# Weight conversions spread over more slots, a low part moved by half an iteration, and output copies moved behind multiplies, in a fused attention and feed-forward kernel

## The chip, the cores and the metric

The kernel runs on one core of one Trainium2 chip. The metric is the device time of one execution in microseconds (us); lower is better. Times are medians of several executions of the same kernel on the same chip.

## The reference

The input is attention data (4 batches, 8 heads, 768 positions, 64 channels), and the output has 3072 rows of 512 numbers. Weights arrive as 64-bit floats and are used as 32-bit floats.

```
for each chunk of 32 queries:
    keys, values = 8 memory rows + 16 rows to the left, the chunk, 8 rows to the right
    a = softmax(q k^T / sqrt(64));  out = a v
x  = out, heads side by side                  # 3072 x 512
h  = x @ w_in                                 # 512 -> 2048
g  = where(h > 0, h, exp(min(h, 0)) - 1)
x1 = g @ w_out                                # 2048 -> 512
y  = ((x1 @ w1) * (x1 @ w2)) @ w3 @ w_out2    # 512 -> 1024, product, 1024 -> 1024 -> 512
```

## The kernel before

**Numbers in two parts.** Every operand of a multiply is held as a high part (`hi`, the value rounded to TensorE's reduced 32-bit form, made by ScalarE with a cast) and a low part (`lo`, the value less `hi`, made by VectorE with a subtraction that reads the cast's result). A product is three multiplies, hi·hi, hi·lo and lo·hi (`mm3`, lines 124 to 126).

**The main loop.** The 3072 rows are cut into 8 blocks of 384. For each block j there are 16 iterations, one per 128 columns of w_in; n counts all 128 iterations. In iteration n TensorE makes `mm_h(n)` (twelve multiplies, h into one of two PSUM banks that alternate, lines 124 to 126 with `xhl`) and `mm_x(n-2)` (twelve multiplies, g into four banks, the same lines with `g`). Between them ScalarE makes relu and exp of h (L539, L540), VectorE the maximum that gives g (`elu_max`, L545, which is also the last reader of the h bank), ScalarE the cast of g (`elu_hi`, L549) and VectorE the low part (`elu_lo`, L553). The order on each engine is the order of the program text: each engine takes its instructions one after another, and one that has to wait holds up all behind it.

**Slots.** Twice per iteration `at_step` runs what a table has put into that slot, so there are 32 slots per block. Since iteration 16 these hold two things. One is attention for the blocks to come, in groups G of 128 queries, three per block, by the list `chain` and the slot offsets "slow": `at_first` (every sixth group, memory keys), `at_turn` (transposes of q and k into the PSUM tile PA, L305 and L307), scores, max, sum, norm, flip, values, `at_out` (cast L120 and low part L121 of the block's input `xhl`, read from PA). The other is the preparation of the second network's weights (`Job`, `plan`): raw 64-bit words are loaded, `rebase` (ScalarE, L159), `shift` (VectorE, L163) and `low` (VectorE, L167) make a 32-bit float tile of 128x512, and it is stored to DRAM as hi and lo. There are 8 tiles of w_out2 (`wos`), 16 of w3 (`w3s`), which TensorE also transposes into PA first (`mid_flip`, L419), and 8 pairs of w1 and w2 tiles (`duos`), each of which gives four stored tiles, two of them from differences (`duo_first`, `duo_second`). Hi and lo of these are made by L172 and L175, and by L438 and L439 for the pairs. The two buffers `st` hold what is about to be stored; `store_next`, at the next slot, issues the store on the SP queue, which also carries the raw loads and those of q, k and v.

In the loop over G (after `GM`), a group that is not the first of its block takes a pair while there are any, and otherwise a w_out2 tile; most groups take a w3 tile too. So the pairs are done in the first four of the six blocks (n = 16 to 111, blocks 1 to 6) in which groups are worked on. The last block (block 7) has none.

**The last stage.** A fold of w3 and w_out2 follows, and then 32 iterations, `mm_step`, eight for each of four pairs of blocks. Each makes seven half products of 6 multiplies (`mm_half`, L661 to L663) by a scheme with sums and differences, whose results alternate between the banks y and z, and six `mm_o` of the iteration before (3 multiplies of 512 columns each) into six accumulators: four banks, and for output tiles 4 and 5 the two halves of PA. ScalarE and VectorE (`sub`, L443) make c11 and c22 of the half products; their product's casts (L699) and low parts feed the next iteration's `mm_o`. In the first iteration of a pair the accumulators of the pair before are finished, and `store_out` copies each to SBUF (even tiles on ScalarE, L115; odd ones on VectorE, L117) and stores it. `do(t)` runs `between[t]`, which is `behind`: `mm_o(n - 1, t)` and, in that iteration, `store_out(p - 1, t)`:

```
        mm_half(n, y, "a22", "t4", False, True)
        do(4)
        do(5)
        sub(c11, c11, c12, ALU.mult)
        sub(c22, y, c22, ALU.mult)
```

Of the kernel before, what the change touches and what calls it, by code (L numbers as in the profile page):

```python
# [8 lines left out]
F32 = mybir.dt.float32  # L9
# [10 lines left out]
def tile_kernel(  # L20
# [23 lines left out]
    nc = tc.nc  # L44
# [371 lines left out]

    def mid_flip(job):
        for i in range(KT):
            nc.tensor.transpose(PA[:, 0, i * P:(i + 1) * P], job.f[:, i * P:(i + 1) * P], ident)  # L419
        mid_split(job, PA[:, 0, :])  # L420

    class Duo:

# [5 lines left out]
        def block(self, i, k):  # L429
            return self.jobs[i].f[:, k * 256:(k + 1) * 256]  # L430

        def keep(self, r, fill):
            w = self.stores[r].shape[2]
            part = Job(None, store=self.stores[r])
            part.to = pools["st"].tile([P, 2, 512], F32R, tag="st", name="st")[:, :, 0:w]
            t = part.to[:, 1, :].bitcast(F32)
            src = fill(t)
            nc.scalar.copy(part.to[:, 0, :], src)  # L438
            nc.vector.tensor_tensor(out=part.to[:, 1, :], in0=src, in1=part.to[:, 0, :].bitcast(F32), op=ALU.subtract)  # L439
            stores.append(part)  # L440
# [5 lines left out]
    def duo_plain(duo):  # L446
        duo.keep(0, lambda t: duo.jobs[0].f)

    def duo_first(duo):
        def fill(t):  # L450
            sub(t[:, 0:256], duo.block(1, 0), duo.block(0, 0))
            sub(t[:, 256:512], duo.block(1, 1), duo.block(1, 0))
            return t

        duo.keep(1, fill)

    def duo_second(duo):
        def fill(t):
            sub(t[:, 256:512], duo.block(1, 1), duo.block(1, 0))
            sub(t[:, 0:256], t[:, 256:512], duo.block(0, 0), ALU.add)  # L460
            sub(t[:, 256:512], duo.block(0, 1), t[:, 0:256])
            return t

        duo.keep(2, fill)

    def duo_last(duo):
        duo.keep(3, lambda t: duo.block(1, 1))

    def store_next():
        while stores:  # L470
# [24 lines left out]
    def plan(s0, job, *steps):  # L495
        mid_jobs.append(job)
        for at, fn in steps:
            put(s0 + at, fn, job)

    for G in range(GPB, NG):  # L500
# [5 lines left out]
        if G % GPB and duos:  # L506
            duo = duos.pop(0)
            plan(s0, duo.jobs[0], (0, rebase), (1, mid_low))
            plan(s0, duo.jobs[1], (2, rebase), (3, mid_low))
# [76 lines left out]
    def fill(slot, src):  # L586
        nc.sync.dma_start(out=W[slot].bitcast(F32), in_=src)
# [77 lines left out]
    def acc(t):  # L665
        return PS[t] if t < KT else PA[:, t - KT, :]

    def mm_step(n, last, between):

        y, z = PS[4][:, 0:TB], PS[5][:, 0:TB]  # L670
        if last:
            for i in sorted(between):
                between[i]()
            return
        r1, r2, r5, c11, c12, c22 = (e_f[i] for i in range(6))
        do = lambda i: between[i]() if i in between else None
# [12 lines left out]
        sub(c22, y, r5, ALU.add)  # L689
        do(3)  # L690
        mm_half(n, z, "s4", "b22", False, True)
        sub(c12, z, r2, ALU.add)
        mm_half(n, y, "a22", "t4", False, True)
        do(4)
        do(5)
        sub(c11, c11, c12, ALU.mult)
        sub(c22, y, c22, ALU.mult)
        for r, e in enumerate((c11, c22)):
            nc.scalar.copy(gq[2 * (n % 2) + r][:, 0, :], e)  # L699
        for r, e in enumerate((c11, c22)):  # L700
            g = gq[2 * (n % 2) + r]
            sub(g[:, 1, :], e, g[:, 0, :].bitcast(F32))
# [15 lines left out]
    with tc.manual_schedule():  # L718
# [40 lines left out]
        for n in range(NH + 2):  # L759
            j, f, at, last = seq[n] if n < NH else (NB, n - NH, n - NH, False)  # L760
            first = at < 2 and n >= 2
            if j == NB - 1 and f == 0:
                store_next()
                mid_ctx.close()
                at_ctx.close()
                late = ctx.enter_context(tc.tile_pool(name="late", bufs=1, side="right"))
                more = [late.tile([P, 2, 2, TB], F32R, name=f"xc{i}") for i in range(3)]
                left.append({})
                for i, what in enumerate(LEFTS[:4]):
                    left[0][what] = [xhl[i // 2][:, r, i % 2 * 2:i % 2 * 2 + 2, :] for r in range(2)]  # L770
                for i, what in enumerate(LEFTS[4:]):
                    left[0][what] = [more[i][:, r] for r in range(2)]
            if n == FF1:
                feed.until(len(feed.jobs) - 1)
                raw_ctx.close()
                mid_ctx = ExitStack()
                pools["raw"] = mid_ctx.enter_context(tc.tile_pool(name="raw2", bufs=2, side="right"))
                pools["st"] = mid_ctx.enter_context(tc.tile_pool(name="st_p", bufs=2, side="right"))
                mid_load(2)

            def x():
                if n >= 2:
                    if n < FF1 + 2:
                        feed.until(due[FF1 + seq[n - 2][1]])
                    mm_x(n - 2)
                    if at == 1 and n < NH:
                        store_x1(j - 1)
                if n < FF1:
                    feed.step()
                at_step()  # L790

            if first:
                x()
            if n < NH:
# [66 lines left out]
        for n in range(NA + 1):  # L861
            p, f = divmod(n, FF2)

            def behind(t, n=n, p=p, f=f):
                if t == 0 and n < NA and p + 1 < NPAIR and f >= 1:
                    left_step(p + 1, f - 1)
                if n >= 1:
                    mm_o(n - 1, t)
                    if f == 0:
                        store_out(p - 1, t)  # L870

            mm_step(n, n == NA, {t: lambda t=t: behind(t) for t in range(2 * GPB)})
# [34 lines left out]
```

## Time and profile before

| what | value |
|---|---|
| median of 3 executions | 1132.85 us (1131.69 to 1133.08) |
| the profiled execution, its own time | 1132.95 us |
| its span, first to last instruction | 1131.1 us |
| TensorE multiplies busy | 1062.1 us, 94% |
| VectorE busy | 593.2 us, 52% |
| ScalarE busy | 461.3 us, 41% |
| instructions in the span | 20839 |

The profile is of one execution. The span is shorter than the time by what lies before the first and after the last instruction. PE is TensorE, DVE is VectorE, ACT is ScalarE, SP is the engine that issues transfers. A line number such as L553 is the line of the kernel; where a helper records an operation, all of its uses share that line. Names such as `xhl<-banks` say which tile an instruction writes and which it reads. An idle time is given with the instruction that ended it.

### The profile page before, as it was taken

How to read it: one execution, taken by the hardware profiler on the slowest of the kernel's cores; microseconds unless marked ns; L12 is line 12 of the kernel's file. 1: busy time of each engine (PE TensorE's matmuls, PEld its weight loads, DVE VectorE, ACT ScalarE, POOL GpSimd, SP SyncE). 2: the span in 40 equal slices, each digit the busy share in tenths (PEclk: the TensorE clock that was granted, in tenths of full speed). 3: DMA queues.
4: the chain of work that ended last, by engine and by line, in shares of the span. 5: the costliest groups of instructions: out<-in, count | busy, mean ns of one | idle time of the engine just before them, and what ended most of it. 6: DMA issues, size and time to landing. Idle time of an engine off the chain costs nothing.

```text
span 1131.1 us, 20839 instructions
## 1 busy us (share of the span) xinstructions
PE 1062.1 (94%) x8528; PEld 996.0 (88%) x8528; DVE 593.2 (52%) x1080; ACT 461.3 (41%) x965; POOL 1.7 (0%) x16
## 2 busy tenths in 40 slices
PE   4788899899899899899999999999999999999998
PEld 4688799799799899799999999789989998998997
DVE  4898566566666566565565334134443443354333
ACT  3667555455455454455444443122222222222122
POOL 0000000000000000000000000000000000000000
PEclk9799999999999999999999999999999999999999
DMA  8947355555554545553421675365465465455531
GB/s 191 297 141 199 94 150 148 161 152 174 163 155 139 166 147 177 162 152 111 139 73 35 196 252 186 129 185 161 152 219 193 144 214 201 148 173 177 177 94 57
DMA packets 170090, 180.40 MB, mean 159 GB/s; under 512 B 101388, under 2 KB 140300, under 8 KB 169996
## 3 DMA queue, kind: packets, MB, share of 16 engines
q1 hardware_dynamic: 168956, 178.81, 51.3%
q8 instruction: 67, 1.10, 0.4%
q10 hardware_dynamic: 1040, 0.26, 0.1%
q14 instruction: 27, 0.22, 0.1%
HBM read 139.20 MB, written 39.85 MB: 158 GB/s over the span
## 4 chain that ended last, share of the span: by engine, by line
PE 62%; DVE 18%; ACT 13%; issue 4%; DMA 3%; DVEq 0%; SPq 0%; ACTq 0%
PE bank L124 11%; PE bank L125 11%; PE bank L126 11%; PE bank L661 7%; PE bank L662 7%; PE bank L663 7%; ACT g L549 3%; DVE eg L545 3%; PE banks L124 2%; DVE e L366 2%; PE banks L126 2%; PE banks L125 2%; DVE pT L377 1%; DVE g L553 1%; ACT eg L540 1%
## 5 line engine op out<-in xcount | busy, mean ns | idle before, releaser
L124 PE MATMUL bank<-xhl,w 128*128 128x384 f32 x512 | 178.7, 349 | 16.4 <-DVE eg L545 15.6
L124 PE MATMUL bank<-g,w 128*128 128x384 f32 x512 | 176.0, 344 | 2.8 <-ACT g L549 2.8
L125 PE MATMUL bank<-xhl,w 128*128 128x384 f32 x512 | 172.8, 337 | 0.9 <-DVE xhl L121 0.9
L126 PE MATMUL bank<-xhl,w 128*128 128x384 f32 x512 | 172.7, 337 | 0.0
L125 PE MATMUL bank<-g,w 128*128 128x384 f32 x512 | 172.1, 336 | 0.3 <-DVE g L553 0.3
L126 PE MATMUL bank<-g,w 128*128 128x384 f32 x512 | 172.0, 336 | 0.0
L549 ACT CAST g<-eg 128x384 fp32r<-128x384 f32 x128 | 65.9, 515 | 168.8 <-DVE eg L545 168.8
L553 DVE TENSOR_TENSOR g<-eg,g 128x384 fp32r<-128x384 f32 x128 | 71.4, 558 | 98.0 <-ACT g L549 98.0
L124 PEld LDWEIGHTS bank<-xhl,w 128*128 128x128 f32 x512 | 97.2, 190 | 24.3 <-DVE eg L545 21.2
L124 PEld LDWEIGHTS bank<-g,w 128*128 128x128 f32 x512 | 96.7, 189 | 4.4 <-ACT g L549 3.2
L125 PEld LDWEIGHTS bank<-xhl,w 128*128 128x128 f32 x512 | 97.2, 190 | 1.3 <-DVE xhl L121 1.3
L125 PEld LDWEIGHTS bank<-g,w 128*128 128x128 f32 x512 | 96.8, 189 | 1.0 <-DVE g L553 1.0
L126 PEld LDWEIGHTS bank<-xhl,w 128*128 128x128 f32 x512 | 97.1, 190 | 0.0
L126 PEld LDWEIGHTS bank<-g,w 128*128 128x128 f32 x512 | 96.5, 189 | 0.0
L545 DVE SCALAR_TENSOR_TENSOR eg<-eg,bank 128x384 f32<-128x384 f32 x128 | 69.6, 544 | 42.9 <-ACT eg L540 42.9
L443 DVE TENSOR_TENSOR e<-bank,e 128x384 f32<-128x384 f32 x64 | 35.4, 554 | 104.9 <-PE bank L663 61.5
L443 DVE TENSOR_TENSOR e<-bank,eg 128x384 f32<-128x384 f32 x64 | 35.7, 558 | 91.8 <-PE bank L663 91.8
L539 ACT ACTIVATE eg<-bank 128x384 f32<-128x384 f32 x128 | 62.7, 490 | 50.7 <-PE bank L126 50.7
L699 ACT CAST g<-e 128x384 fp32r<-128x384 f32 x64 | 31.4, 513 | 126.3 <-DVE e L443 126.3
L661 PE MATMUL bank<-xd,w 128*128 128x384 f32 x224 | 76.1, 340 | 3.5 <-DVE e L443 3.5
L662 PE MATMUL bank<-xd,w 128*128 128x384 f32 x224 | 76.7, 342 | 0.0
L663 PE MATMUL bank<-xd,w 128*128 128x384 f32 x224 | 76.4, 341 | 0.0
(143 smaller groups left out, 1870.9 us busy)
## 6 DMA issues: line engine op xcount, KB each, us to landing
w<-wqd SPq DMA_DIRECT2D x96, 512.0 KB
raw<-in_moe_w_dram SPq DMA_DIRECT2D x32, 512.0 KB
wqd<-st SPq DMA_DIRECT2D x24, 512.0 KB
raw<-in_moe_w_out_dram SPq DMA_DIRECT2D x20, 512.0 KB
w3d<-st SPq DMA_DIRECT2D x16, 512.0 KB
w<-w3d SPq DMA_DIRECT2D x16, 512.0 KB
w<-wqd SPq DMA_DIRECT2D x32, 256.0 KB
raw<-in_moe_w_in_dram SPq DMA_DIRECT2D x12, 512.0 KB
```

Source lines behind the costliest of these rows:

```text
L124: mm(o, lhsT=w_hi, rhs=x_hi, start=start, stop=False)
L125: mm(o, lhsT=w_hi, rhs=x_lo, start=False, stop=False)
L126: mm(o, lhsT=w_lo, rhs=x_hi, start=False, stop=stop)
L443: nc.vector.tensor_tensor(out=o, in0=a, in1=b, op=op)
L539: nc.scalar.activation(e, h_t[n], AF.Relu, scale=-1.0)
L545: nc.vector.scalar_tensor_tensor(out=e, in0=e, scalar=-1.0, in1=h_t.pop(n), op0=ALU.add, op1=ALU.max)
L549: nc.scalar.copy(g_t[n][:, 0, :], eg_t[n])
L553: nc.vector.tensor_tensor(out=g[:, 1, :], in0=eg_t.pop(n), in1=g[:, 0, :].bitcast(F32), op=ALU.subtract)
L661: mm(o, lhsT=args[0], rhs=args[2], start=start and i == 0, stop=False, skip_group_check=more)
L662: mm(o, lhsT=args[0], rhs=args[3], start=False, stop=False, skip_group_check=more)
L663: mm(o, lhsT=args[1], rhs=args[2], start=False, stop=i == 1, skip_group_check=more)
L699: nc.scalar.copy(gq[2 * (n % 2) + r][:, 0, :], e)
```

## The change

Four things are edited; no operation is added or left out.

1. `shift` is no longer part of `mid_low`, and hi and lo of a converted tile are separate steps: `mid_hi`, `mid_lo`, `mid_flip_lo`, and for the pairs `Duo.hi` and `Duo.lo`. The two differences now only write `duo.next`; their hi and lo follow as steps.
2. The slots are written out anew (`plan_duo` and the two `plan` lines), and the list DUOS says which groups, counted from the first, take a pair: over all six blocks. The other groups take w_out2 tiles.
3. `elu_lo` of iteration n-1 comes in iteration n, behind the first slot, instead of directly behind `elu_hi`.
4. In the last stage, copies and stores of output tiles 4 and 5 come behind both `mm_o` and behind c22 and c11, which are exchanged. At the very end tile 5 is stored before tile 4.

```diff
     def mid_low(job):
-        shift(job)
         low(job)
         mid_load(mid_jobs.index(job) + 3)
 
-    def mid_split(job, src=None):
-        job.to = pools["st"].tile([P, 2, 512], F32R, tag="st", name="st")
+    def mid_hi(job, src=None):
+        job.to = st_tile()
         hi_of(job, src)
-        lo_of(job, src)
+
+    def mid_lo(job):
+        lo_of(job)
         stores.append(job)
 
     def mid_flip(job):
         for i in range(KT):
             nc.tensor.transpose(PA[:, 0, i * P:(i + 1) * P], job.f[:, i * P:(i + 1) * P], ident)
-        mid_split(job, PA[:, 0, :])
+        mid_hi(job, PA[:, 0, :])
+
+    def mid_flip_lo(job):
+        lo_of(job, PA[:, 0, :])
+        stores.append(job)
...
-            for at, fn in ((2, duo_plain), (7, duo_first), (8.5, duo_last), (9.5, duo_second)):
-                put(s0 + at, fn, duo)
...
+    def plan_duo(s0, duo):
+        plan(s0, duo.jobs[0], (-1, rebase), (0.1, shift), (0.2, mid_low))
+        plan(s0, duo.jobs[1], (1, rebase), (1.3, shift), (2.3, mid_low))
...
+            (10.3, duo_second), (10.4, lambda d: d.hi(2)), (11.1, Duo.lo),
...
+    DUOS = (1, 2, 4, 7, 10, 11, 13, 16)
...
         elif wos:
-            plan(s0, wos.pop(0), (0, rebase), (1, mid_low), (2, mid_split))
-        if w3s and (not G % GPB or len(duos) % 4 < 3):
-            plan(s0, w3s.pop(0), (4, rebase), (5, mid_low), (9, mid_flip))
+            plan(s0, wos.pop(0), (2, rebase), (3.5, shift), (4.5, mid_low), (5.1, mid_hi), (6.1, mid_lo))
+        if w3s and G - GM not in (2, 11):
+            plan(s0, w3s.pop(0), (5, rebase), (6.2, shift), (7.6, mid_low), (9.1, mid_flip), (9.6, mid_flip_lo))
...
+        def do(i):
+            between[i]()
+            if i < 4:
+                stored(i)
+
...
         do(4)
         do(5)
+        sub(c22, y, c22, ALU.mult)
         sub(c11, c11, c12, ALU.mult)
-        sub(c22, y, c22, ALU.mult)
+        stored(4)
+        stored(5)
...
             at_step()
             if spread:
                 elu_exp(n)
+            if FF1 < n < NH:
+                elu_lo(n - 1)
             if not first:
                 x()
             if n < NH:
                 elu_max(n)
             if n < NH and not spread:
                 elu_hi(n)
-                elu_lo(n)
+                if n == NH - 1:
+                    elu_lo(n)
```

How the instructions stand now, at three places. Lines have moved by some: L545 is now L555, L553 is L563, L439 of the pairs is L175, L443 is L455.

VectorE, third group of block 1, from the transpose of the softmax (L377) on; L545 is elu_max, L553 the lo of g, L121 the lo of the attention output, and the `st` rows are the pair and the flipped w3 tile. Before:

```order
L377 STREAM_TRANSPOSE pT<-e_2440 128x1024
L443 TENSOR_TENSOR st<-f 128x256 x2
L439 TENSOR_TENSOR st<-st 128x512
L545 SCALAR_TENSOR_TENSOR eg<-eg,bank_95 128x384
L553 TENSOR_TENSOR g<-eg,g 128x384
L121 TENSOR_TENSOR xhl_73<-banks,xhl_73 128x2x4x64
L439 TENSOR_TENSOR st<-f,st 128x256
L175 TENSOR_TENSOR st<-banks,st 128x512
L443 TENSOR_TENSOR st<-f 128x256
L443 TENSOR_TENSOR st<-st,f 128x256
L443 TENSOR_TENSOR st<-f,st 128x256
L439 TENSOR_TENSOR st<-st 128x512
```

and with the change:

```order
L377 STREAM_TRANSPOSE pT<-e_2454 128x1024
L455 TENSOR_TENSOR st<-f 128x256 x2
L563 TENSOR_TENSOR g<-eg,g 128x384
L175 TENSOR_TENSOR st<-st 128x512
L555 SCALAR_TENSOR_TENSOR eg<-eg,bank_95 128x384
L121 TENSOR_TENSOR xhl_73<-banks,xhl_73 128x2x4x64
L563 TENSOR_TENSOR g<-eg,g 128x384
L555 SCALAR_TENSOR_TENSOR eg<-eg,bank_96 128x384
L455 TENSOR_TENSOR st<-f 128x256
L455 TENSOR_TENSOR st<-st,f 128x256
L455 TENSOR_TENSOR st<-f,st 128x256
L175 TENSOR_TENSOR st<-st 128x512
```

The lo of g now stands ahead of the max instead of behind it, there is no flip in this group, and the block's last max (bank_96) stands ahead of the second difference instead of behind it.

ScalarE, block 1, from the end of its first group to the turn of its second (L309 copies the turned q); L120 is the cast of the attention output, `st<-banks` the cast of the flipped w3 tile, L159 a rebase. Before:

```order
L120 CAST xhl_73<-banks 128x2x4x64
L549 CAST g<-eg 128x384
L539 ACTIVATE eg<-bank_96 128x384
L540 ACTIVATE eg<-eg 128x384
L172 CAST st<-banks 128x512
L309 COPY qT<-banks 128x512
```

and with the change:

```order
L120 CAST xhl_73<-banks 128x2x4x64
L559 CAST g<-eg 128x384
L549 ACTIVATE eg<-bank_96 128x384
L550 ACTIVATE eg<-eg 128x384
L159 ACTIVATE f<-raw 128x512
L172 CAST st<-banks 128x512
L309 COPY qT<-banks 128x512
```

The rebase of the next pair's first tile now stands ahead of the flip's cast.

VectorE, first iteration of a pair in the last stage; `st<-banks` is the copy of output tile 5, `e_8035` is c11, `e_8037` is c22, bank_95 is y. Before:

```order
L117 COPY st<-banks 128x512
L443 TENSOR_TENSOR e_8035<-e_8035,e_8036 128x384
L443 TENSOR_TENSOR e_8037<-bank_95,e_8037 128x384
L443 TENSOR_TENSOR g<-e_8035,g 128x384
L443 TENSOR_TENSOR g<-e_8037,g 128x384
```

and with the change:

```order
L455 TENSOR_TENSOR e_8037<-bank_95,e_8037 128x384
L455 TENSOR_TENSOR e_8035<-e_8035,e_8036 128x384
L117 COPY st<-banks 128x512
L455 TENSOR_TENSOR g<-e_8035,g 128x384
L455 TENSOR_TENSOR g<-e_8037,g 128x384
```

c22, the last reader of y, and then c11 now stand ahead of the copy.

## Rows read from the trace of the kernel before

**Rows 1.** The page, first part: busy time, share of the span, instructions.

```profile
PE 1062.1 (94%) x8528; PEld 996.0 (88%) x8528; DVE 593.2 (52%) x1080; ACT 461.3 (41%) x965; POOL 1.7 (0%) x16
```

**Rows 2.** Table by stage, blocks 1-7: length; PE, PEld, DVE, ACT, POOL; clock; DMA.

```profile
132.62:213.91 81.29, 78.63 (x803) 75.26 (x801) 49.85 (x95) 41.97 (x93) 0.00 (x0) 1.00 0.50 151
213.91:299.52 85.61, 80.08 (x810) 75.51 (x809) 53.84 (x104) 43.27 (x93) 0.00 (x0) 1.00 0.54 163
299.52:382.45 82.93, 78.86 (x802) 75.17 (x801) 52.23 (x100) 42.60 (x94) 0.00 (x0) 1.00 0.51 153
382.45:467.96 85.51, 80.34 (x809) 75.46 (x808) 53.77 (x103) 43.10 (x93) 0.00 (x0) 1.00 0.54 163
467.96:549.57 81.61, 79.44 (x807) 76.87 (x805) 47.13 (x88) 40.52 (x90) 0.00 (x0) 0.98 0.46 135
549.57:628.45 78.88, 78.19 (x805) 75.33 (x805) 41.57 (x77) 37.23 (x82) 0.00 (x0) 1.00 0.27 76
628.45:694.90 66.45, 66.45 (x385) 66.45 (x385) 21.20 (x37) 27.09 (x53) 0.00 (x0) 1.00 0.70 234
```

**Rows 3.** TensorE's waits, 132.6 to 628.5: us in total, times, longest.

```profile
PE banks L419 <- DVE xhl L121: 6.4, 4, 1.6
PE bank L124 <- DVE eg L545: 5.9, 11, 0.8
PE banks L305 <- ACT memo L300: 3.8, 2, 2.2
PE bank L124 <- ACT g L549: 2.8, 2, 1.6
PE banks L305 <- DVE st L175: 0.6, 3, 0.2
```

**Rows 4.** Waits of all engines, whole span, same columns.

```profile
DVE g L553 <- ACT g L549: 98.0, 114, 3.6
```

**Rows 5.** Timeline, end of block 1: start, us, instruction, idle time before it.

```profile
208.03 0.55 DVE L545 SCALAR_TENSOR_TENSOR eg<-eg,bank 128x384 f32<-128x384 f32 x1
...
208.61 0.51 ACT L549 CAST g<-eg 128x384 fp32r<-128x384 f32 x1 [1.22 <-DVE eg L545]
...
210.58 0.69 DVE L121 TENSOR_TENSOR xhl<-banks,xhl 128x512 fp32r<-128x512 f32 x1 [0.86 <-ACT xhl L120]
...
211.32 0.33 PE L419 MATMUL banks<-ident,f 128*128 128x128 f32 x1 [1.61 <-DVE xhl L121]
```

**Rows 6.** Timeline, turn of a second group (block 2); then L159's group.

```profile
244.08 0.33 PE L305 MATMUL banks<-ident,qn 128*128 128x128 f32 x1 [0.20 <-DVE st L175]
...
L159 ACT ACTIVATE f<-raw 128x512 f32<-128x512 f32 x64 | 42.9, 670 | 0.4 <-DMA raw<-in_moe_w_dram 0.4
```

**Rows 7.** Table by stage: iterations of the last stage at pair boundaries, and one plain.

```profile
831.55:846.02 14.47, 11.98 (x61) 10.48 (x60) 5.20 (x10) 3.69 (x8) 0.00 (x0) 0.98 0.52 197
846.02:860.45 14.43, 14.43 (x61) 13.47 (x61) 5.09 (x10) 3.64 (x8) 0.00 (x0) 0.79 0.66 221
860.45:872.00 11.55, 11.55 (x61) 10.75 (x60) 4.61 (x10) 3.15 (x6) 0.00 (x0) 1.00 0.48 159
944.24:957.47 13.23, 13.23 (x61) 12.43 (x61) 5.09 (x10) 3.64 (x8) 0.00 (x0) 0.87 0.75 239
1041.26:1052.92 11.66, 11.66 (x60) 10.86 (x61) 4.22 (x9) 2.92 (x7) 0.00 (x0) 1.00 0.79 270
```

**Rows 8.** Timeline at the first pair boundary.

```profile
842.65 0.59 ACT L115 COPY st<-banks 128x512 f32<-128x512 f32 x1 [4.02 <-PE banks L126]
...
843.29 0.51 PE L124 MATMUL banks<-w,g 128*128 128x512 f32 x1 [0.72 <-ACT st L115]
...
844.34 0.69 DVE L117 COPY st<-banks 128x512 f32<-128x512 f32 x1 [2.91 <-PE banks L126]
...
846.02 0.69 PE L661 MATMUL bank<-xd,w 128*128 128x384 f32 x1 [1.77 <-DVE e L443]
```

**Rows 9.** Timeline, last output tile.

```profile
1126.54 0.50 PE L124 MATMUL banks<-w,g 128*128 128x512 f32 x1 [0.72 <-ACT st L115]
```

More of the change, by code (lines that the diff above doesn't have):

```diff
@@ L406, in mid_low, with st_tile @@
     def mid_low(job):
-        shift(job)
         low(job)
         mid_load(mid_jobs.index(job) + 3)
-    def mid_split(job, src=None):
-        job.to = pools["st"].tile([P, 2, 512], F32R, tag="st", name="st")
+    def st_tile(w=512):
+        return pools["st"].tile([P, 2, 512], F32R, tag="st", name="st")[:, :, 0:w]
+    def mid_hi(job, src=None):
+        job.to = st_tile()
         hi_of(job, src)
-        lo_of(job, src)
+    def mid_lo(job):
+        lo_of(job)
         stores.append(job)
@@ L430, in block, with hi, lo @@
             return self.jobs[i].f[:, k * 256:(k + 1) * 256]
-        def keep(self, r, fill):
+        def hi(self, r, src=None):
             w = self.stores[r].shape[2]
[L434 to L440, printed above, removed]
+            self.part = Job(None, store=self.stores[r])
+            if src is None:
+                self.part.to, src = self.next, self.next[:, 1, :].bitcast(F32)
+            else:
+                self.part.to = st_tile(w)
+            self.src = src
+            hi_of(self.part, src)
+        def lo(self):
+            lo_of(self.part, self.src)
+            stores.append(self.part)
     def sub(o, a, b, op=ALU.subtract):
@@ L444, in sub @@
         return o
-    def duo_plain(duo):
-        duo.keep(0, lambda t: duo.jobs[0].f)
     def duo_first(duo):
[L450 to L455, printed above, removed]
-    def duo_second(duo):
[L458 to L467, printed above, removed]
+        duo.next = st_tile()
+        t = duo.next[:, 1, :].bitcast(F32)
+        sub(t[:, 0:256], duo.block(1, 0), duo.block(0, 0))
+        sub(t[:, 256:512], duo.block(1, 1), duo.block(1, 0))
+    def duo_second(duo):
+        duo.next = st_tile()
+        t = duo.next[:, 1, :].bitcast(F32)
+        sub(t[:, 256:512], duo.block(1, 1), duo.block(1, 0))
+        sub(t[:, 0:256], t[:, 256:512], duo.block(0, 0), ALU.add)
+        sub(t[:, 256:512], duo.block(0, 1), t[:, 0:256])
     def store_next():
@@ L498, in plan @@
             put(s0 + at, fn, job)
+    def plan_duo(s0, duo):
+        plan(s0, duo.jobs[0], (-1, rebase), (0.1, shift), (0.2, mid_low))
+        plan(s0, duo.jobs[1], (1, rebase), (1.3, shift), (2.3, mid_low))
+        for at, fn in (
+            (1.2, lambda d: d.hi(0, d.jobs[0].f)), (2.2, Duo.lo),
+            (4.5, lambda d: d.hi(3, d.block(1, 1))), (5.1, Duo.lo),
+            (6.8, duo_first), (6.9, lambda d: d.hi(1)), (7.5, Duo.lo),
+            (10.3, duo_second), (10.4, lambda d: d.hi(2)), (11.1, Duo.lo),
+        ):
+            put(s0 + at, fn, duo)
+    DUOS = (1, 2, 4, 7, 10, 11, 13, 16)
     for G in range(GPB, NG):
@@ L505, in tile_kernel @@
             continue
[L506 to L509, printed above, removed]
-            for at, fn in ((2, duo_plain), (7, duo_first), (8.5, duo_last), (9.5, duo_second)):
-                put(s0 + at, fn, duo)
+        if G - GM in DUOS:
+            plan_duo(s0, duos.pop(0))
         elif wos:
-            plan(s0, wos.pop(0), (0, rebase), (1, mid_low), (2, mid_split))
-        if w3s and (not G % GPB or len(duos) % 4 < 3):
-            plan(s0, w3s.pop(0), (4, rebase), (5, mid_low), (9, mid_flip))
+            plan(s0, wos.pop(0), (2, rebase), (3.5, shift), (4.5, mid_low), (5.1, mid_hi), (6.1, mid_lo))
+        if w3s and G - GM not in (2, 11):
+            plan(s0, w3s.pop(0), (5, rebase), (6.2, shift), (7.6, mid_low), (9.1, mid_flip), (9.6, mid_flip_lo))
     assert not wos and not w3s and not duos, (len(wos), len(w3s), len(duos))
@@ L666, in acc, with mm_step @@
         return PS[t] if t < KT else PA[:, t - KT, :]
-    def mm_step(n, last, between):
+    def mm_step(n, last, between, stored):
         y, z = PS[4][:, 0:TB], PS[5][:, 0:TB]
@@ L673, in mm_step @@
                 between[i]()
+                if i != 4:
+                    stored(i)
+            stored(4)
             return
         r1, r2, r5, c11, c12, c22 = (e_f[i] for i in range(6))
-        do = lambda i: between[i]() if i in between else None
+        def do(i):
+            between[i]()
+            if i < 4:
+                stored(i)
         mm_half(n, y, "a11", "b11", True, True)
@@ L695, in mm_step @@
         do(5)
+        sub(c22, y, c22, ALU.mult)
         sub(c11, c11, c12, ALU.mult)
-        sub(c22, y, c22, ALU.mult)
+        stored(4)
+        stored(5)
         for r, e in enumerate((c11, c22)):
@@ L868, in behind, with stored @@
                     mm_o(n - 1, t)
-                    if f == 0:
-                        store_out(p - 1, t)
-            mm_step(n, n == NA, {t: lambda t=t: behind(t) for t in range(2 * GPB)})
+            def stored(t, p=p, f=f, n=n):
+                if n >= 1 and f == 0:
+                    store_out(p - 1, t)
+            mm_step(n, n == NA, {t: lambda t=t: behind(t) for t in range(2 * GPB)}, stored)
             if n < NA:
```

## The prediction

> **What bounds the kernel now.** I read the page's first part, then the table by stage, then who made TensorE wait, then the timeline at the longest waits. TensorE is busy for 94% of the span and VectorE for 52% [rows 1], so only TensorE's idle time can be won, and only where another engine causes it. The sum is made against the profiled execution, 1132.95 us with a span of 1131.1 us; the median of the three runs is 1132.85, so the two differ by 0.1 and I do not correct for it.
>
> The floor of the main loop can be read from its last block, which has no attention and no weight conversion: 384 multiplies in 66.45 us [rows 2] (the row's 385 counts one that reaches in), so 173 ns each, and 2.08 us for a run of twelve (one mm_h or one mm_x). The six blocks before it, in which attention and conversions run beside the multiplies, last 81.29, 85.61, 82.93, 85.51, 81.61 and 78.88 us [rows 2], 495.8 together. The sixth has the fewest conversions and is the shortest, though all six make nearly the same multiplies: what differs is waiting.
>
> Who is waited for [rows 3]: in this stretch TensorE waited 6.4 us for VectorE's lo of the attention output before it could flip a w3 tile, 5.9 for elu_max to give a bank back, 3.8 for ScalarE's copy of the memory keys, 2.8 for ScalarE's cast of g, 0.6 for the lo of the flip. That is 19.5 us in 22 waits. A multiply is drawn 0.33 us long while the next can start 0.17 after it, so the view misses 0.16 per wait: 3.5 more. One wait is followed by a stretch at 1.2 instead of 2.4 GHz; the fifth block's mean granted clock of 0.98 over 81.61 us makes this 1.6 us at most, and I take 1.5. Together 24.5 us.
>
> What these waits have in common is the loop VectorE–ScalarE–VectorE. At the end of the first block [rows 5], ScalarE starts the cast of g only at 208.61, when VectorE has finished the max that began at 208.03; only behind that cast come the relu of the next tile, the cast of the attention output, its lo on VectorE (210.58) and the flip on TensorE at 211.32, 1.61 us late. VectorE is not full there; it is held up. In the old order each lo stands directly behind its own cast, and VectorE stands still meanwhile: 98.0 us for the lo of g alone, 114 times [rows 4].
>
> In the last stage an iteration takes 11.55 us [rows 7]. Where a pair of blocks ends it takes 14.47 (three times, one row shown), and the iteration after it 14.43, 13.23 and 11.66, with the granted clock at 0.79, 0.87 and 1.00. The 14.47 is seen in the timeline [rows 8]: the multiplies of output tile 5 wait 0.72 for ScalarE's copy of tile 4, which lies in the same PSUM tile; VectorE's copy of tile 5 (844.34) stands ahead of the two products c11 and c22, and the next iteration's first multiply waits 1.77 for c22, which reads the bank it writes. VectorE had been idle for 2.91 us before that copy.
>
> **The change, part by part.** Nothing is added or removed: every operation of before is there again, with the same shape, so the busy times stay.
>
> *Output tiles 4 and 5.* Both are now copied after both are multiplied, so the 0.72 goes. c22 and c11 are emitted before the copies, and c22 first: it can run in the 2.91 us in which VectorE was idle, and the 1.77 goes too. What is late next? ScalarE's copy of tile 4 (0.59 [rows 8]) and VectorE's copy of tile 5 (0.69) now stand ahead of the casts and los of g, one after the other, since one PSUM tile is read by both. From the end of tile 5 the first cast is done on ScalarE at 0.59 + 0.51 (the cast of g in [rows 5] has its shape), and the first lo follows VectorE's copy at some 1.4 and is done at 2.0 (0.55, as the max of that shape in [rows 5]); the multiply that reads it comes after two halves of six multiplies, 2.08, and two more, at least 0.34. Some 0.4 is left, so I put this at nothing; without this cover it would cost up to 0.6 three times. In the other iterations c11 comes 0.55 later, hidden by the same 2.4 us. So each boundary iteration becomes 11.55: 3 × 2.92 = 8.8. With TensorE no longer stopped, nothing lowers its clock: 2.88 + 1.68 + 0.11 = 4.7. At the very end the 0.72 and its 0.16 [rows 9] go, but the copy of tile 4 now runs behind that of tile 5 (0.59 and a handover): 0.2. Sum of the end: **13.7 us**.
>
> *Conversions and the low part of g.* Shift, low, cast and lo now lie in slots of their own, half an iteration or more apart, and the los of g come half an iteration later, so VectorE should hardly wait for ScalarE. The second difference of a column pair leaves the last slot of a block's third group; before, its three subtractions, cast and lo stood between the flip and the max that all later work needed. Eight column pairs are spread over six blocks instead of four. On SP, stores and raw loads keep their order relative to each other nearly everywhere, and a raw load is still asked for two tiles ahead; no TensorE wait of before was for a DMA in this stretch. I therefore take all 24.5 us away, and then put back what the new order makes.
>
> The place where it makes a wait is the slot before at_turn of a block's second group. There ScalarE rebases the new pair's first tile *ahead of* the cast of the flipped w3 tile. Before, the turn's transposes already waited 0.20 + 0.16 there for the lo of the flip [rows 6]. A rebase is 0.67 us [rows 6]. If all else stays, the wait becomes 1.03; if the relu ahead starts some 0.4 sooner because the previous max is no longer late, 0.65. I take 0.85, six times: 5.1 (bounds 3.9 and 6.2). For small waits that I don't see, 1 us. Middle: 24.5 − 5.1 − 1 = **18.4 us**. As a second way: if all six blocks took the sixth's 78.88, 22.5 would go; less the added 0.49 six times, 19.6.
>
> One rule speaks against this part. The waits for casts sum to 98.0 us on VectorE [rows 4] but only some 20 us reach TensorE [rows 3], so the price of a wait on VectorE is a matter of place. The Trainium skill, "VectorE: DVE Perf Modes", section "Rules for kernel authors", says of chained operations to lower their number, not their semaphores. By that rule the middle would win nothing, as the number of operations stays. The rule is about one engine's own chain; here the wait is for another engine, and the trace shows VectorE idle for 0.86 us each time (98.0 over 114).
>
> **The forecast.** 1132.95 − 13.7 − 18.4 = 1100.85, so **1101 us**.
>
> **The rivals.**
> 1. *The middle's waits only change place.* VectorE's work per block is the same, 41.6 to 53.8 us [rows 2], and a max held back in the old order may be held back somewhere else in the new one. Then only the end is won: 1132.95 − 13.7 = 1119. For it: the fall of a wait at the flip may bring out the one at the turn, and blocks five and six get a pair each that they did not have. Against it: the sixth block, with four conversions and no pair, lasts 78.88, so conversions as such don't hold a max back. Chance 0.12. (By the rule quoted, it would be this one.)
> 2. *The clock falls at the pair boundaries all the same*, since the loads for the next pair start there. Then 4.7 us stay: 1105.5. Against it: TensorE stops before each fall, and even the third boundary, with the same stop, has a clock of 1.00 behind it [rows 7]: loads alone, which all three have, don't lower it. Chance 0.05.
> 3. *Slower: the later lo of g is too late.* It now stands behind the slot's VectorE work. The multiply that needs it starts two runs later, 4.2 us. If VectorE runs behind TensorE by more than that, each of some 95 iterations waits. From 0.14 us an iteration on, this eats the end's 13.7; at 0.5 us the time is 1132.95 − 13.7 + 47.5 = 1167. Against it: VectorE is idle for 37% even in the fullest block [rows 2]. Chance 0.02.
>
> No change at all would need the gains and rival 3 to cancel: 0.01. Better than my bounds: 0.04. What is left for the forecast is 0.76.
>
> **Range and chances.** Best case: no price at the turn, and waits too short for the view go as well, some 26 us in the middle: 1093. Worst case of the forecast: half of the middle's gain (8 to 9), or rival 2 with a poor middle: 1111 to 1112. Range **1093 to 1112**; rival 1, the better tail and rival 3 lie outside (0.19). About 0.2% (2.3 us) is what a measurement of this kernel can tell from no change. Faster by more: 0.76 + 0.12 + 0.05 + 0.04 = 0.97; same 0.01; slower 0.02.
>
> **What would show it.** In the profile after: the lo of g waiting under 15 us in all instead of 98.0; no flip waiting for the lo of the attention output; the boundary iterations at 11.55 and the clock at 1.00 in the last stage; the six blocks at 78 to 80 us each; and transposes of the turn waiting some 0.7 us six times for the lo of the flip. I am wrong if the six blocks still sum to over 488 us, or if elu_max is again named as what gives the banks back late.

## The result, and the profile after

The changed kernel takes **1092.7 us** (median of 4 runs, 1092.39 to 1092.9) where the kernel before takes 1132.96 on the same chips: a ratio of 0.9646, 95% interval 0.9629 to 0.9662. The forecast was 1101 with a range of 1093 to 1112. The direction and the mechanism came out, the size did not: 40.3 us were won, 32.1 forecast (13.7 + 18.4), and the time lies 0.3 us below the range.

The page of the profile after, first part (its execution took 1092.9 us, the span is 1091.1 us); it answers to [rows 1]:

```profile
PE 1049.1 (96%) x8528; PEld 991.6 (91%) x8528; DVE 581.9 (53%) x1080; ACT 458.5 (42%) x965; POOL 1.7 (0%) x16
```

The busy times are nearly what they were. The table by stage with the seven blocks (columns as in [rows 2]):

```profile
132.73:210.47 77.74, 77.38 (x803) 74.94 (x802) 49.73 (x99) 42.80 (x95) 0.00 (x0) 1.00 0.57 171
210.47:288.97 78.50, 78.14 (x810) 75.39 (x809) 47.95 (x94) 41.32 (x90) 0.00 (x0) 1.00 0.53 154
288.97:367.13 78.16, 77.80 (x806) 75.33 (x805) 47.59 (x93) 41.18 (x92) 0.00 (x0) 1.00 0.53 152
367.13:445.20 78.07, 77.71 (x805) 74.99 (x804) 49.71 (x99) 42.05 (x91) 0.00 (x0) 1.00 0.55 164
445.20:523.39 78.19, 77.83 (x806) 75.36 (x805) 48.19 (x94) 41.70 (x93) 0.00 (x0) 1.00 0.52 153
523.39:601.47 78.08, 77.72 (x806) 75.25 (x806) 44.38 (x87) 39.26 (x86) 0.00 (x0) 1.00 0.34 100
601.47:667.90 66.43, 66.43 (x385) 66.43 (x385) 21.00 (x37) 27.07 (x53) 0.00 (x0) 1.00 0.70 234
```

The six blocks with attention last 77.7 to 78.5 us each, 468.7 together where they took 495.8 [rows 2]: 27.1 us won. The seventh is unchanged. Of TensorE's waits in the six blocks [rows 3] one kind is left, and VectorE's waiting for the cast of g [rows 4] has shrunk to 16.9 us (the prediction named under 15 as a sign). TensorE's waits from 132.7 to 601.5 (us, times, longest):

```profile
PE banks L305 <- DVE st L175: 2.2, 6, 0.4
```

The waits of all engines of the same kernel, over the whole span (same columns):

```profile
DVE g L563 <- ACT g L559: 16.9, 21, 3.2
```

In the last stage the boundary iteration and the one behind it take what a plain one takes, at a clock of 1.00, where [rows 7] had 14.47 and 14.43 (the first boundary):

```profile
804.56:816.11 11.55, 11.55 (x61) 10.75 (x60) 5.11 (x9) 3.41 (x7) 0.00 (x0) 1.00 0.58 224
816.11:827.67 11.56, 11.56 (x62) 10.75 (x60) 5.10 (x9) 3.62 (x8) 0.00 (x0) 1.00 0.84 299
```

From the first half product to the end of the span this stage took 1131.13 − 742.35 = 388.8 us and takes 1091.12 − 715.37 = 375.7: 13.0 won. With the 27.1, and 0.1 lost ahead of the blocks, that is the whole difference of the spans, 40.0.

### The profile page after: what moved, and what is told of

Read it like the earlier page. It is cut to its first block, busy times and chain, and to the rows that moved or that the text cites. A ratio compares the mean times of both kernels' runs of the same rounds, so it can differ in the third digit from the quotient of the medians.

```text
span 1091.1 us, 20849 instructions
## 1 busy us (share of the span) xinstructions
PE 1049.1 (96%) x8528; PEld 991.6 (91%) x8528; DVE 581.9 (53%) x1080; ACT 458.5 (42%) x965; POOL 1.7 (0%) x16
## 4 chain that ended last, share of the span: by engine, by line
PE 86%; DVE 6%; ACT 5%; issue 1%; DMA 1%; SPq 0%; ACTq 0%; DVEq 0%
PE bank L124 18%; PE bank L125 18%; PE bank L126 18%; PE bank L672 7%; PE bank L673 7%; PE bank L671 7%; PE banks L388 2%; PE banks L126 2%; PE banks L125 2%; PE banks L124 2%; PE banks L329 1%; DVE w L175 1%; PE banks L305 1%; ACT w L172 1%; ACT f L159 1%
## 5 line engine op out<-in xcount | busy, mean ns | idle before, releaser
L124 PE MATMUL bank<-xhl,w 128*128 128x384 f32 x512 | 178.2, 348 | 10.6 <-DVE eg L555 9.8
L555 DVE SCALAR_TENSOR_TENSOR eg<-eg,bank 128x384 f32<-128x384 f32 x128 | 70.1, 548 | 55.7 <-ACT eg L550 55.7
L455 DVE TENSOR_TENSOR e<-bank,e 128x384 f32<-128x384 f32 x64 | 35.7, 558 | 118.9 <-PE bank L673 76.6
L563 DVE TENSOR_TENSOR g<-eg,g 128x384 fp32r<-128x384 f32 x128 | 70.7, 552 | 16.9 <-ACT g L559 16.9
L672 PE MATMUL bank<-xd,w 128*128 128x384 f32 x224 | 75.8, 338 | 0.0
L673 PE MATMUL bank<-xd,w 128*128 128x384 f32 x224 | 75.6, 337 | 0.0
L671 PE MATMUL bank<-xd,w 128*128 128x384 f32 x224 | 74.9, 334 | 0.0
L550 ACT ACTIVATE eg<-eg 128x384 f32<-128x384 f32 x128 | 67.3, 526 | 4.1
```

Source lines behind the costliest of these rows:

```text
L124: mm(o, lhsT=w_hi, rhs=x_hi, start=start, stop=False)
L550: nc.scalar.activation(e, e, AF.Exp, scale=-1.0)
L555: nc.vector.scalar_tensor_tensor(out=e, in0=e, scalar=-1.0, in1=h_t.pop(n), op0=ALU.add, op1=ALU.max)
L563: nc.vector.tensor_tensor(out=g[:, 1, :], in0=eg_t.pop(n), in1=g[:, 0, :].bitcast(F32), op=ALU.subtract)
L671: mm(o, lhsT=args[0], rhs=args[2], start=start and i == 0, stop=False, skip_group_check=more)
L672: mm(o, lhsT=args[0], rhs=args[3], start=False, stop=False, skip_group_check=more)
```

## The experiments

The edits are called *slots* (first and second), *lo* (third) and *end* (fourth). "Six blocks" is the stretch from block 1's first multiply to block 7's, read from the table by stage; the columns are those of [rows 2].

**One edit at a time.** Each of these is the kernel before with one of the edits, except the last, which is the changed kernel with lo undone:

```diff
             if n < NH and not spread:
                 elu_hi(n)
-                if n == NH - 1:
-                    elu_lo(n)
+                elu_lo(n)
```

> The kernel before with only the fourth edit (copies of output tiles 4 and 5 behind both multiplies, c22 ahead of c11). Theory: the end is a matter of its own. The stage from the first half product to the end was 388.8 us before and is 375.8 after, so this run is 13.0 below before (1119.9), its plain and boundary iterations are all 11.55 us, the clock in the last stage is 1.00, and the six blocks still sum to 495.8. Rival: the clock in the last stage falls because of the loads of the next pair; then half-clock stretches stay here and the run is only some 8.5 below before (1124.4).

> The kernel before with only the first two edits (the conversions' slots), the lo of g directly behind its cast as before and the old end. Theory: the long waits came from where the conversions stood, above all the second difference in a block's last slot, so this takes most of the six blocks' 27.1 us: sum 472 to 478, time 1109 to 1115. Rival: it is the lo of g standing behind its cast that holds VectorE up, and the slots alone give little: sum 486 or more, time 1123 or more.

> The kernel before with only the third edit (lo of g half an iteration later), old slots, old end. Theory: VectorE's 98.0 us of waiting for the cast of g falls under 30, but the flips and the second difference still hold the max back at the ends of blocks: the six blocks sum to 486 to 492, time 1123 to 1129. Rival: this edit alone is most of the gain: sum under 478, time under 1115.

> The changed kernel with the lo of g put back directly behind its cast. Theory: the new slots leave enough room on VectorE that most of its waiting for the cast is covered: 3 to 8 us above the changed kernel (1096 to 1101), and VectorE waits some 80 us or more for the cast of g. Rival (the lo is what counts): 12 us or more above, 1105 or more.

| run | median us | before, same chip | ratio, 95% interval |
|---|---|---|---|
| end alone | 1120.42 | 1131.77 | 0.9896 (0.9875 to 0.9917) |
| slots alone | 1103.76 | 1131.77 | 0.9752 (0.9727 to 0.9778) |
| lo alone | 1129.13 | 1131.77 | 0.9977 (0.9964 to 0.999) |
| all but lo | 1092.71 | 1131.77 | 0.9652 (0.9632 to 0.9672) |

The kernel before scatters from 1129 to 1135 us over its runs here; the changed kernel and most of its variants repeat within 0.7 us. So kernels that differ by a few us are compared below by their own medians, and the intervals of the ratios are mostly the scatter of before. The changed kernel was not run again beside them, so a difference of a us or two is read from the lengths of the stages: where the code of a stage is the changed kernel's, its length agrees within 0.1 us between the traces (six blocks 468.70 to 468.76, last stage 375.72 to 375.79).

The six blocks of "end alone", "slots alone", "lo alone" and "all but lo", one row from the table by stage of each run:

```profile
132.31:628.52 496.21, 475.62 (x4827) 453.59 (x4825) 298.38 (x566) 248.29 (x544) 0.00 (x0) 1.00 0.47 141
```

```profile
132.06:600.82 468.76, 466.56 (x4827) 451.26 (x4825) 294.71 (x566) 248.76 (x544) 0.00 (x0) 1.00 0.51 149
```

```profile
132.49:626.10 493.61, 472.75 (x4826) 450.43 (x4825) 292.44 (x566) 248.00 (x544) 0.00 (x0) 1.00 0.47 142
```

```profile
132.32:601.07 468.75, 466.57 (x4827) 451.27 (x4826) 294.70 (x566) 248.74 (x544) 0.00 (x0) 1.00 0.51 149
```

End alone leaves the six blocks as they were (496.2 against 495.8) and has the last stage of the changed kernel, 375.8 us at a clock of 1.00: as expected, and the rival on the clock falls. Slots alone gives the six blocks their whole 27 us, to 0.02 us what the changed kernel has; I had expected most of it, not all. That makes lo worthless here, and "all but lo" says so directly: it is as fast as the changed kernel, though VectorE stands still for the cast of g nearly as long as before (waits of all engines, "all but lo"):

```profile
DVE g L563 <- ACT g L559: 88.2, 114, 3.3
```

My expectation for that run (3 to 8 us slower) was wrong, and so was its rival. In the old slots lo alone wins a little, 2.2 us of the six blocks, less than the 4 to 10 that I had expected. VectorE's waiting for the cast falls to 25.6 us, as expected, but a wait grows that hardly existed before (0.3 us in two waits): the multiply that reads the lo of g comes too early for it (TensorE's waits, "lo alone"):

```profile
PE bank L125 <- DVE g L553: 9.9, 7, 2.2
```

**Which part of the slots.** Two things changed there: the steps (cast and lo in slots of their own, the second difference later, and other slots for nearly all of them) and the choice of groups (pairs over six blocks). The first run keeps the new steps and takes the old choice, the second the reverse:

```diff
-        if G - GM in DUOS:
+        if G % GPB and duos:
             plan_duo(s0, duos.pop(0))
...
-        if w3s and G - GM not in (2, 11):
+        if w3s and (not G % GPB or len(duos) % 4 < 3):
```

```diff
-            plan(s0, wos.pop(0), (2, rebase), (3.5, shift), (4.5, mid_low), (5.1, mid_hi), (6.1, mid_lo))
+            plan(s0, wos.pop(0), (0, rebase), (1, shift), (1, mid_low), (2, mid_hi), (2, mid_lo))
...
-            (10.3, duo_second), (10.4, lambda d: d.hi(2)), (11.1, Duo.lo),
+            (9.5, duo_second), (9.5, lambda d: d.hi(2)), (9.5, Duo.lo),
```

> The changed kernel with the new steps but the old choice of groups: the column pairs go to groups two and three of the first four blocks, as before, and w3 tiles to the groups that had them. Theory A (what counts is that cast and lo, and the second difference, have slots of their own): at most 4 us above the changed kernel, 1092.5 to 1097, six blocks at 469 to 473. Theory B (what counts is that the pairs are spread over six blocks): 8 us or more above, 1101 or more.

> The changed kernel with the new choice of groups but the old steps: shift with low, cast with lo in one slot, the second difference in slot 9.5. Theory A: the waits come back wherever a pair stands, in two blocks as the second difference ahead of the last max; six blocks at 480 to 488, 1104 to 1112. Theory B: six blocks under 476, under 1100.

New steps with the old choice: 1091.71 us (ratio 0.9652, 0.9637 to 0.9666, to 1130.64 before). Old steps with the new choice: 1108.84 us (0.9799, 0.9784 to 0.9814). The six blocks of each:

```profile
132.47:600.10 467.63, 466.19 (x4826) 451.25 (x4825) 288.13 (x566) 249.40 (x544) 0.00 (x0) 1.00 0.51 150
```

```profile
132.09:617.27 485.18, 472.55 (x4826) 452.43 (x4825) 291.83 (x566) 248.12 (x544) 0.00 (x0) 1.00 0.48 144
```

Theory A holds, and further than I had put it: with the new steps the choice of groups is worth nothing, the old one is even 1.1 us shorter in the six blocks (two waits of the turn fewer, as there are four where the changed kernel has six). With the old steps 16.4 us come back, mostly in the form of the wait that lo alone had made (TensorE's waits, old steps with the new choice):

```profile
PE bank L125 <- DVE g L563: 10.6, 8, 2.0
PE bank L124 <- DVE eg L555: 1.3, 2, 0.6
```

"Lo alone" has the old steps and the old choice, with lo moved as in these two runs; so the six blocks can be set side by side. With the old choice the new steps win 26.0 us (493.6 to 467.6), with the new choice 16.4 (485.2 to 468.7). The new choice wins 8.4 while the steps are old (493.6 to 485.2), and nothing once they are new. The spreading is thus a weaker remedy for the same waits. Whether the new steps help because the halves stand apart, or because they stand in other slots, no run tells.

**The second difference.** One number changed in the kernel before, and the three steps put back in the changed kernel:

```diff
-            for at, fn in ((2, duo_plain), (7, duo_first), (8.5, duo_last), (9.5, duo_second)):
+            for at, fn in ((2, duo_plain), (7, duo_first), (8.5, duo_last), (10.3, duo_second)):
```

```diff
-            (10.3, duo_second), (10.4, lambda d: d.hi(2)), (11.1, Duo.lo),
+            (9.5, duo_second), (9.55, lambda d: d.hi(2)), (9.57, Duo.lo),
```

> The kernel before with a single number changed: the second difference of a pair one slot later (10.3 for 9.5), out of the block's last slot. Theory: of the 30 us of waiting in the six blocks the part at the blocks' ends and starts that hangs on it goes (waits of the turn for the memory keys and of mm_x for the cast of g, 3.8 and 2.8 in the view), so 5 to 9 us under before: 1123 to 1127. Rival: the max comes late by the first difference just as well, and it gains under 2 us.

> The changed kernel with the second difference, its cast and its lo put back into one slot at 9.5. Two of the eight pairs stand in a block's third group, so there, at the ends of the first and fourth block, the max comes late again: 3 to 6 us above the changed kernel (1095.5 to 1099), in those two blocks and the starts of the next. Rival: with no flip in these two groups the max has room, and it costs under 1 us.

The first: 1127.55 us against 1130.64 (0.9966, 0.9953 to 0.9979), so some 3 us, less than expected. The waits that I had tied to it did go, the turn's for the memory keys and mm_x's for the cast of g, but the max then gave its banks back late more often (TensorE's waits; elu_max had 5.9 us in 11 waits before [rows 3]):

```profile
PE bank L124 <- DVE eg L545: 11.5, 16, 1.5
```

The second: 1093.85 us, 1.2 above the changed kernel, neither the 3 to 6 expected nor the under 1 of the rival. It is not where I looked for it either: the six blocks are 1.7 longer, and TensorE waits only for the lo of the flip at a turn, eight times instead of six.

```profile
PE banks L305 <- DVE st L175: 3.1, 8, 0.6
```

So the second difference was not the culprit; the other steps were not taken out one by one. In both single changes of the old order, this one and lo alone, the waits that went were partly replaced by others; all the new steps together leave only the turn's.

**The end.** In the first run tile 4 is copied before tile 5 is multiplied, at the three pair boundaries (the edit does not reach the fourth place, the very end); in the second c11 and c22 stand behind both copies:

```diff
             between[i]()
-            if i < 4:
+            if i <= 4:
                 stored(i)
...
-        stored(4)
         stored(5)
```

```diff
-        sub(c22, y, c22, ALU.mult)
-        sub(c11, c11, c12, ALU.mult)
         stored(4)
         stored(5)
+        sub(c11, c11, c12, ALU.mult)
+        sub(c22, y, c22, ALU.mult)
```

> The changed kernel, but output tile 4 is copied before tile 5 is multiplied, as it was before; c22 and c11 still stand ahead of the copy of tile 5. So the 0.72 us wait for ScalarE's copy is back and the 1.77 us wait for c22 stays away. Theory: each of four places costs 0.72 to 0.9 again and the clock stays at 1.00, so some 3 to 3.5 us above the changed kernel (1096). Rival on the clock: any stop at a pair boundary lets the clock fall while the next pair's loads run; then up to 4.7 more, 1100 or more.

> The changed kernel, but c11 and c22 stand behind the copies of tiles 4 and 5, in the order of before. So the first wait is gone, and VectorE's copy, which waits for ScalarE's copy of the same PSUM tile, stands ahead of c22. Theory: one wait of 2.0 to 2.8 us for c22 at each of three boundaries, 6 to 8.5 us above the changed kernel, and a granted clock under 1.00 behind at least one of them for up to 5 more: 1099 to 1106. Rival: the copies are hidden behind the multiplies of the two tiles and it makes no difference, under 1094.

They take 1095.51 us (0.9669, 0.9652 to 0.9685, to 1133.31) and 1101.67 us (0.9721, 0.9698 to 0.9745), 2.8 and 9.0 above the changed kernel, close to the first expectation (1096) and inside the second (1099 to 1106). Boundary iteration and the next one; first with tile 4 copied early, then with c11 and c22 last, and there also the iteration behind the second and the third boundary:

```profile
803.75:816.29 12.54, 11.82 (x61) 10.67 (x60) 5.11 (x9) 4.82 (x10) 0.00 (x0) 1.00 0.54 205
816.29:827.85 11.56, 11.56 (x62) 10.75 (x60) 5.19 (x9) 2.31 (x5) 0.00 (x0) 1.00 0.85 300
```

```profile
803.73:817.82 14.09, 11.71 (x61) 10.56 (x60) 5.21 (x10) 3.69 (x8) 0.00 (x0) 1.00 0.54 204
817.82:831.03 13.21, 13.21 (x61) 12.36 (x61) 5.10 (x10) 3.65 (x8) 0.00 (x0) 0.87 0.74 241
914.44:927.46 13.02, 13.02 (x60) 12.22 (x61) 5.09 (x10) 3.65 (x8) 0.00 (x0) 0.88 0.71 242
1010.87:1022.53 11.66, 11.66 (x61) 10.85 (x61) 4.23 (x9) 2.92 (x7) 0.00 (x0) 1.00 0.80 272
```

TensorE's waits at the three boundaries in each (first run, then second):

```profile
PE banks L124 <- ACT st L115: 2.2, 3, 0.7
```

```profile
PE bank L671 <- DVE e L455: 7.1, 3, 2.4
```

A wait of 0.72 makes the iteration 0.99 longer, 3.0 in three, and leaves the clock at 1.00, while the next pair's loads run at the same time (DMA share 0.85). A wait of 2.4 makes it 2.54 longer, and behind two of three the clock is 0.87 and 0.88, with less load traffic. So the loads alone do not lower the clock, and each fall in these rows came behind a long stop of TensorE; but the third boundary, with the same stop of 2.4, shows that the stop does not lower it every time.

**The wait that was left.** The pair's first rebase goes behind the flip's cast; and in a second run c11 stands ahead of c22 again in the last iteration only:

```diff
-        plan(s0, duo.jobs[0], (-1, rebase), (0.1, shift), (0.2, mid_low))
+        plan(s0, duo.jobs[0], (-0.8, rebase), (0.1, shift), (0.2, mid_low))
```

```diff
+        if n == NA - 1:
+            sub(c11, c11, c12, ALU.mult)
         sub(c22, y, c22, ALU.mult)
-        sub(c11, c11, c12, ALU.mult)
+        if n < NA - 1:
+            sub(c11, c11, c12, ALU.mult)
```

> The changed kernel, but the rebase of a pair's first tile stands behind the cast of the flipped w3 tile on ScalarE instead of ahead of it, in the same slot. The six waits of the transposes for the lo of the flip are listed with 2.2 us in all, and each costs 0.52 from start to start. Theory: a rebase of 0.67 in front is the whole of that wait, so all six go and the run is 3.1 us below the changed kernel (1089.6). Rival: the chain max, cast of g, relu, exp ahead of it is as late, and at most half of it goes: 1091 or more.

> As the run with the rebase behind the cast, and in the very last iteration c11 stands ahead of c22 as before, since there no half products lie between the product and the multiply that reads its cast. Theory: the 0.27 us wait for the cast of g at the end (0.43 from start to start) goes too: 0.4 below the run with the rebase alone, 1089.2. Rival: the cast is then late for the lo, or y's last reader late for the end, and nothing changes.

1089.32 us (0.9614, 0.9597 to 0.963, to 1133.31) and **1088.76 us** (0.9609, 0.9592 to 0.9625). The first is 3.4 below the changed kernel (3.1 expected) and its six blocks are 3.3 shorter, with no wait of TensorE left that the view lists. The second is the fastest kernel of this study, 0.6 below the first in the medians and 0.7 in the last stage (375.7 to 375.0 us), where 0.4 was expected. The old choice of groups together with these two edits was not tried.

```profile
132.10:597.57 465.47, 465.47 (x4827) 451.30 (x4826) 287.60 (x566) 248.56 (x544) 0.00 (x0) 1.00 0.51 150
```

## Why the prediction missed its range, point by point

**The end: 13.7 forecast, 13.0 measured.** The boundaries came out as worked out: 11.55 us each, no fall of the clock, 13.4. The timeline of the changed kernel at the first boundary shows why (start, us, instruction, idle time before it):

```profile
814.92 0.56 DVE L455 TENSOR_TENSOR e<-bank,e 128x384 f32<-128x384 f32 x1 [0.48 <-PE bank L673]
815.40 0.55 DVE L455 TENSOR_TENSOR e<-e,e 128x384 f32<-128x384 f32 x1
816.98 0.69 DVE L117 COPY st<-banks 128x512 f32<-128x512 f32 x1 [1.03 <-ACT st L115]
...
816.36 0.59 ACT L115 COPY st<-banks 128x512 f32<-128x512 f32 x1 [4.71 <-PE banks L126]
...
816.11 0.33 PE L671 MATMUL bank<-xd,w 128*128 128x384 f32 x1
```

c22 (814.92) and c11 (815.40) run while tiles 4 and 5 are multiplied, the next half product starts at 816.11 without a wait, and the copies follow, VectorE's behind ScalarE's, as forecast. The copies at the very end gained 0.3 (forecast 0.2; from the start of the last iteration on, before took 20.44 us and the run with c11 first takes 20.15). What I had not seen: c11 behind c22 is hidden "in the other iterations" by two half products, but the last iteration has none behind it. There the multiply waits for the cast of g; with what follows, this costs 0.7 in all, which the run with c11 first gives back:

```profile
1082.27 0.50 PE L124 MATMUL bank<-w,g 128*128 128x512 f32 x1 [0.27 <-ACT g L719]
```

**The middle: 18.4 forecast, 27.1 measured.** This is the step that failed, and all of its three terms were mis-sized in the same direction; the direction itself, TensorE's waits going away, was right.

- *What the old order lost: 24.5 in the text, 30.4 in fact* (495.8 less the 465.5 of the run without any wait there). I compared the starts of all the multiplies in these blocks, kind by kind, between the trace of before and that run. The waits that the view lists (24 of them; [rows 3] leaves out two of 0.15 for the lo of g) cost 23.8, idle time and the 0.16 or so by which each multiply is drawn too long, close to the 23.0 that I had taken for them. The half-clock stretch cost 1.6, where I had taken 1.5. But 1.8 were lost in the first step *behind* the waits, and 3.2 in places that the view does not name: half of it slower small multiplies of the attention (L388; why they are slower is open), half seven delays with under 0.13 us of idle time each. Even my best case had allowed only 1.5 for all that the view does not show. One such restart in the trace of before; the steps are 0.28, 0.18 and 0.18 where 0.17 is usual:

```profile
203.86 0.45 PE L124 MATMUL bank<-xhl,w 128*128 128x384 f32 x1 [0.48 <-DVE eg L545]
204.14 0.34 PE L125 MATMUL bank<-xhl,w 128*128 128x384 f32 x1
204.32 0.35 PE L126 MATMUL bank<-xhl,w 128*128 128x384 f32 x1
204.50 0.34 PE L124 MATMUL bank<-xhl,w 128*128 128x384 f32 x1
```

- *What the new order makes: 5.1 for the turn's wait, 3.3 in fact.* It is where I said, six times, but 0.55 from start to start, below my lower bound of 0.65. The relu ahead does start some 0.4 sooner, as the lower bound had it: 0.20 behind the flip's first multiply (156.84 to 157.04), where it was 0.59 at the turn of [rows 6]. What was priced too high is the rebase, which pushes the cast back by 0.56 from start to start (157.99 to 158.55) and not by its drawn 0.67; the rest is that I took the middle between my bounds. First the two rows of before, then the changed kernel's, which end in the wait that [rows 6] had at 0.20:

```profile
241.19 0.60 PE L419 MATMUL banks<-ident,f 128*128 128x128 f32 x4
...
241.78 0.49 ACT L539 ACTIVATE eg<-bank 128x384 f32<-128x384 f32 x1
```

```profile
156.84 0.60 PE L423 MATMUL banks<-ident,f 128*128 128x128 f32 x4
...
156.62 0.51 ACT L559 CAST g<-eg 128x384 fp32r<-128x384 f32 x1 [1.22 <-DVE eg L555]
157.04 0.49 ACT L549 ACTIVATE eg<-bank 128x384 f32<-128x384 f32 x1
...
157.99 0.65 ACT L159 ACTIVATE f<-raw 128x512 f32<-128x512 f32 x1
158.55 0.57 ACT L172 CAST st<-banks 128x512 fp32r<-128x512 f32 x1
...
159.15 0.69 DVE L175 TENSOR_TENSOR st<-banks,st 128x512 fp32r<-128x512 f32 x1 [2.56 <-ACT st L172]
...
159.89 0.33 PE L305 MATMUL banks<-ident,qn 128*128 128x128 f32 x1 [0.36 <-DVE st L175]
```

- *One us for small waits:* there were none.

So 30.4 − 3.3 = 27.1. My second way of counting, with the sixth block of before as the measure, gave 19.6 for the same reason: that block still had waits.

**Who did it.** The text took the loop VectorE–ScalarE–VectorE as the cause and gave the same weight to the lo of g and to the conversions. Half of this is wrong. The lo of g, whose 98.0 us of waiting [rows 4] the text leaned on, cost nothing that its move could still win once the slots were new: undone there, it changes the time by 0.0; in the old slots it won 2.2. The conversions' steps are enough for all of it, and the spreading over six blocks, which I counted among the reasons, adds nothing to them (8.4 us where the steps are old). The sentence that the price of a wait on VectorE is a matter of place was right and should have been applied to the lo itself. Of the lo the rule named from the Trainium skill ("VectorE: DVE Perf Modes", "Rules for kernel authors") gave the right answer, no gain (0.0 us in the new slots); of the conversions, whose number stayed too, it did not (27.1 us).

**The rivals.** The first (waits only change place) and the second (the clock falls all the same) did not happen to the whole change; what the first describes did happen to single edits, the second difference and lo alone, which won 2.5 and 2.2 us in the six blocks. The third's mechanism, the lo of g too late for its multiply, is real: it is there, with 9.9 and 10.6 us, in both runs in which lo is moved and the steps are not separated. With separated steps no wait of this kind is listed for TensorE. It costs less there than the old waits did, so it would not have made the kernel slower.

## What to carry to other kernels

A pair of steps in which one engine must wait for the other (a cast, then the low part) should not stand in one place of an in-order queue when something else can stand between them; here giving such steps slots of their own won 26.0 us without any spreading, and spreading without it 8.4. The sum of an engine's waiting says nothing about its price: look for the wait at which the bounding engine stops, and test a suspect by undoing it. When several late steps feed the same waits, removing one can move the time to the next, so single removals can add up to far less than the whole (2.5 and 2.2 us here, against 27.1); and an engine's listed waits are a lower bound of what it loses to them (19.6 us listed here, 30.4 lost).

## What the runs showed of the hardware that I had not expected

A stop of TensorE costs more than the idle time that the profile lists: here 24 waits with 19.6 us of idle time were worth 25.6. Of the difference about 4 is in how the profile draws a multiply (0.33 us long, the next 0.17 behind it), and 1.8 is a slow restart: in the rows shown above the second multiply starts 0.28 behind the first instead of 0.17. The granted clock of the iteration behind a pair boundary was 1.00 where the stop was 0.72 us. Where it was 2.4 us, the clock was 0.87, 0.88 and 1.00 behind three equal stops of one execution, so it fell to 1.2 GHz for a part of the first two and not in the third.
